# Retention and a squared-ReLU layer: the decay of q moved into GpSimd's cast, the retention outputs as plain copies by two engines

## Chip, cores, metric

One Trainium2 chip, one core. The metric is the device time of one execution in microseconds (us), lower is better.

## What is computed

```python
def attn_ref(q, k, v):            # (8, 8, 576, 64): batch, heads, sequence, head size
    scores = (1 / sqrt(64)) * q @ k.transpose(0, 1, 3, 2)
    gamma = 1 - 2.0 ** (-5 - arange(8))                 # one decay per head
    rel = pos[:, None] - pos[None, :]
    Dmat = where(rel >= 0, gamma[:, None, None] ** rel, 0)
    return (scores * Dmat) @ v

x = attn_ref(q, k, v).transpose(0, 2, 1, 3).reshape(4608, 512)
out = maximum(x @ w_in, 0) ** 2 @ w_out                 # w_in 512 x 2048, w_out 2048 x 512
```

Since gamma^(i-j) = gamma^i * gamma^-j, the decay can be applied as one factor on the side of the row i (q, or the finished output of row i) and one on the side of the column j (v).

## The kernel before

The work is cut into 36 units of 128 rows, taken in pairs (groups). Units 0 to 7 go another way that the change doesn't touch. A schedule written in Python runs through all tasks with assumed durations and emits each engine's instructions in the order that comes out, so a change of a task's engine or duration can also move other instructions.

GpSimd (POOL) casts k and q to float16 and multiplies v by its decay; a DMA transposes k and q:

```python
        def fq():
            sorted_cast(nc.gpsimd.tensor_copy, tile_of["kq", u][:, 1], tile_of["q32", u])

        def fv():
            t = tile_of["v16", u] = cast.tile([P, H, D], FP16, name="v16", tag="v16")
            nc.gpsimd.tensor_tensor(
                out=t, in0=tile_of["v32", u],
                in1=vdec[kind].rearrange("p (h o) -> p h o", o=1).to_broadcast([P, H, D]), op=ALU.mult)
        ...
        cq = add("POOL", base + 1, 0.62, fq, deps=[loaded["q", u], ck])
```

TensorE (PE) leaves the outputs of a pair in `psO`, a PSUM tile of two banks (`[P, 2, 512]`); the two units are the two halves of the columns. VectorE (DVE) takes both out and applies the row's decay:

```python
        for u in us:
            ...
                nc.vector.tensor_tensor(
                    out=tile_of["x", g][:, :, s * P:(s + 1) * P].rearrange("p n (c i) -> p c n i", c=2),
                    in0=tile_of["psO", g][:, :, cols(at)].rearrange("p c (n i) -> p c n i", i=64),
                    in1=gam[units[u][0]], op=ALU.mult)
```

`xT` then goes through the first product (`ph`), ScalarE's ReLU (`rl`), and the square (`gT`, on ScalarE or VectorE). The second product (`po`) is done with seven partial products instead of eight, for which VectorE makes sums and differences of squares, with two inputs in SBUF:

```python
                    nc.vector.tensor_tensor(out=Sx(k, h), in0=in0(h), in1=in1(h), op=op)   # gS
```

## Time and profile before

| | |
|---|---|
| median of 3 runs | 292.55 us (292.39 to 292.78) |
| span of the profiled run | 290.9 us, TensorE clock 1.0 |
| TensorE, VectorE, ScalarE, GpSimd busy | 283.0, 195.0, 187.5, 88.9 us |

A line of the timeline or the chain starts with its start and length in us. A line of the groups has, after the first bar, the busy time in us and the mean of one instruction in ns, then the idle time of the engine before them and what ended it. Matmuls overlap, so the distance from start to start tells more than busy time. Where this document speaks of steps, it is that distance on TensorE, and "lost" is what exceeds the median for its kind.

### The profile page before, as it was taken

Reading aid. Unit: us, or ns where it says so; the run is one execution under the profiler, and the core shown is the slowest. Engines: PE = TensorE matmul, PEld = TensorE weight load, DVE = VectorE, ACT = ScalarE, POOL = GpSimd, SP = SyncE. Lnnn points to the kernel's source line nnn. Section 1 sums busy time; section 2 is a strip of 40 time slices with the busy share of each in tenths; the row PEclk is TensorE's granted clock in tenths of the full one; section 3 lists DMA queues with packets and bytes.
Section 4 is the critical chain, followed back from the end, with each engine's and each line's share of the span. In section 5 each row is a group of like instructions: output and inputs, shape, how many; then the busy total and the mean of one; then the engine's idle time right before and its main releaser. Section 6 shows DMA issues by size and latency. Waiting matters only on the chain.

```text
span 290.9 us, 10062 instructions
## 1 busy us (share of the span) xinstructions
PE 283.0 (97%) x4328; PEld 234.0 (80%) x4328; DVE 195.0 (67%) x430; ACT 187.5 (64%) x354; POOL 88.9 (31%) x123
## 2 busy tenths in 40 slices
PE   7989999999999999999999999999999999999994
PEld 2557765688888888888888888888888888888883
DVE  3796589748485848656868857667786865565632
ACT  6456966296757575867666666766767676747830
POOL 5343454524434234251616041615151400000000
PEclk9999999999999999999999999999999999999999
DMA  7999999999999899997998599979896820201004
GB/s 201 327 368 387 370 276 250 239 220 186 233 214 214 185 148 247 221 186 189 196 208 180 126 192 211 202 183 180 211 188 171 159 74 2 74 3 72 2 2 144
DMA packets 139421, 54.13 MB, mean 186 GB/s; under 512 B 118129, under 2 KB 130929, under 8 KB 139377
## 3 DMA queue, kind: packets, MB, share of 16 engines
q1 hardware_dynamic: 139072, 53.23, 81.9%
q8 instruction: 34, 0.56, 0.9%
q10 hardware_dynamic: 304, 0.26, 0.3%
q14 instruction: 11, 0.08, 0.1%
HBM read 36.70 MB, written 9.44 MB: 159 GB/s over the span
## 4 chain that ended last, share of the span: by engine, by line
PE 89%; DMA 6%; SPq 1%; issue 1%; POOL 1%; DVE 0%; DVEq 0%; POOLq 0%
PE ph L827 42%; PE po L916 34%; PE po L865 5%; PE psO L343 4%; DMA wi<-in_moe_w_in_dram 3%; DMA pair<-in_q_dram 3%; PE psc L343 2%; PE psS L343 2%; SPq L298 1%; POOL w_in L322 1%; PE psT L418 1%; DVE o L939 0%; POOL qx L403 0%; DVE p L968 0%; DVEq L939 0%
## 5 line engine op out<-in xcount | busy, mean ns | idle before, releaser
L827 PE MATMUL ph<-xT,w_in 128*128 128x256 f16 x1152 | 139.4, 273 | 0.2 <-POOL w_in L322 0.2
L827 PEld LDWEIGHTS <-w_in 128*128 128x128 f16 x1152 | 111.1, 98 | 14.8 <-POOL w_in L322 0.4
L835 ACT ACTIVATE rl<-ph 128x512 f16<-128x512 f32 x144 | 84.3, 589 | 46.9 <-PE ph L827 45.0
L845 ACT ACTIVATE gT<-rl 128x512 f16<-128x512 f16 x104 | 65.6, 631 | 3.0
L916 PEld LDWEIGHTS <-gS 128*128 128x128 f16 x512 | 49.4, 98 | 6.1 <-DVE gS L893 0.2
L916 PE MATMUL po<-wT,gS 128*128 128x256 f16 x384 | 52.4, 273 | 0.0
L893 DVE TENSOR_TENSOR gS<-gT,gS 128x512 f16<-128x512 f16 x64 | 35.1, 554 | 11.6 <-ACT gT L845 11.0
L916 PEld LDWEIGHTS <-gT 128*128 128x128 f16 x384 | 37.2, 98 | 4.4
L893 DVE TENSOR_TENSOR gS<-gT 128x512 f16<-128x512 f16 x64 | 30.7, 481 | 12.9 <-ACT gT L845 12.9
L916 PE MATMUL po<-w_out,gT 128*128 128x256 f16 x256 | 34.5, 273 | 0.0
L355 POOL CAST kq<-q 128x512 f16<-128x512 f32 x28 | 18.8, 673 | 45.7 <-DMA q<-in_q_dram 45.5
L367 POOL TENSOR_TENSOR v<-v,vdec_full 128x512 f16<-128x512 f32 x24 | 26.2, 1093 | 19.6 <-DMA v<-in_v_dram 14.4
L355 POOL CAST kq<-k 128x512 f16<-128x512 f32 x28 | 18.6, 666 | 44.4 <-DMA k<-in_k_dram 41.7
L847 DVE TENSOR_TENSOR gT<-rl 128x512 f16<-128x512 f16 x40 | 18.9, 473 | 14.7 <-ACT rl L835 14.2
L929 ACT COPY u<-po 128x256 f32<-128x256 f32 x32 | 11.8, 369 | 20.4 <-PE po L916 20.4
L939 DVE TENSOR_TENSOR o<-po,u 128x256 f32<-128x256 f32 x31 | 13.0, 421 | 16.2 <-PE po L916 8.3
L704 DVE TENSOR_TENSOR xT<-psO,gam_full 128x512 f16<-128x512 f32 x28 | 18.9, 686 | 7.5 <-PE psO L343 7.4
L643 DVE TENSOR_TENSOR rT<-psc,mask 128x512 f16<-128x512 f32 x28 | 18.3, 683 | 5.5 <-PE psc L343 5.2
L916 PE MATMUL po<-w_out,gS 128*128 128x256 f16 x128 | 17.0, 273 | 0.0
L916 PE MATMUL po<-wT,gT 128*128 128x256 f16 x128 | 16.8, 273 | 0.0
L939 DVE TENSOR_TENSOR o<-po,p 128x256 f32<-128x256 f32 x17 | 7.2, 424 | 13.7 <-ACT u L929 7.1
L865 PE MATMUL po<-w_out,gT 128*128 128x512 f16 x64 | 15.8, 380 | 0.0
(81 smaller groups left out, 244.1 us busy)
## 6 DMA issues: line engine op xcount, KB each, us to landing
out_dram<-o SPq DMA_DIRECT2D x31, 256.0 KB, 3.0
k<-in_k_dram SPq DMA_DIRECT2D x24, 256.0 KB, 4.5
q<-in_q_dram SPq DMA_DIRECT2D x24, 256.0 KB, 4.8
v<-in_v_dram SPq DMA_DIRECT2D x24, 256.0 KB, 5.3
wi<-in_moe_w_in_dram SPq DMA_DIRECT2D x4, 1024.0 KB, 10.1
wo<-in_moe_w_out_dram SPq DMA_DIRECT2D x4, 1024.0 KB, 9.7
pair<-in_k_dram SPq DMA_DIRECT2D x4, 512.0 KB, 7.0
pair<-in_q_dram SPq DMA_DIRECT2D x4, 512.0 KB, 7.0
```

The source lines that it names most:

```text
L343: nc.tensor.matmul(out_, lhsT=lhsT, rhs=rhs, start=start, stop=True, skip_group_check=True, tile_position=(64 * row, 64 * col))
L355: op(out=out_.rearrange("p (n b a d) -> p n b a d", n=2, b=2, a=2), in_=in_.rearrange("p (n a b) d -> p n b a d", n=2, a=2))
L367: nc.gpsimd.tensor_tensor(out=t, in0=tile_of["v32", u], in1=vdec[kind].rearrange("p (h o) -> p h o", o=1).to_broadcast([P, H, D]), op=ALU. ...
L704: nc.vector.tensor_tensor(out=tile_of["x", g][:, :, s * P:(s + 1) * P].rearrange("p n (c i) -> p c n i", c=2), in0=tile_of["psO", g][:, :, ...
L827: nc.tensor.matmul(tile_of["ph", g, fb][:, j, :], lhsT=w_in16[:, m, fi * P:(fi + 1) * P], rhs=tile_of["x", g][:, m, :], start=(m == 0), st ...
L835: nc.scalar.activation(out=t, in_=tile_of["ph", g, fb], func=ACTF.Relu)
L845: nc.scalar.activation(out=t, in_=rl, func=ACTF.Square)
L847: nc.vector.tensor_tensor(out=t, in0=rl, in1=rl, op=ALU.mult)
L865: nc.tensor.matmul(tile_of["po", u], lhsT=tile_of["g", g][:, fi, s * P:(s + 1) * P], rhs=w_out16[:, fi, :], start=(fi == 0), stop=(fi == N ...
L893: nc.vector.tensor_tensor(out=Sx(k, h), in0=in0(h), in1=in1(h), op=op)
L916: nc.tensor.matmul(tile_of["pb", g, bank], lhsT=left(i), rhs=right[:, i, :], start=(start and i == 0), stop=(i == HF - 1), skip_group_chec ...
L939: nc.vector.tensor_tensor(out=o_tile(u)[:, half * HM:(half + 1) * HM], in0=bank(x), in1=tile_of[name, g], op=ALU.add)
```

## The change

VectorE has 28 multiplications out of PSUM in the changed form. The intent is to apply the row's decay earlier, in GpSimd's cast of q, where GpSimd has time, so that the outputs can leave PSUM as plain copies; then one unit of each pair can go to ScalarE, and the two copies could run side by side.

```diff
-    vdec = {}
+    vdec, qdec = {}, {}
 
     def make_vdec(kind, pos):
         t = const.tile([P, H], FP32, name=f"vdl_{kind}")
         nc.vector.tensor_scalar(out=t, in0=lnrow, scalar1=pos, scalar2=None, op0=ALU.mult)
+        if kind in ("full", "tail"):
+            e = qdec[kind] = const.tile([P, H], FP32, name=f"qdec_{kind}")
+            nc.scalar.activation(out=e, in_=t, func=ACTF.Exp, scale=-1.0)
...
-    gam = {"full": gam_f.rearrange("p n (c i) -> p c n i", c=2),
-           "tail": gam_f[:, :, 0:64].rearrange("p n (c i) -> p c n i", c=1).to_broadcast([P, 2, NP, 64])}
...
         def fq():
-            sorted_cast(nc.gpsimd.tensor_copy, tile_of["kq", u][:, 1], tile_of["q32", u])
+            for n in range(2):
+                nc.gpsimd.tensor_tensor(
+                    out=tile_of["kq", u][:, 1].rearrange("p (n b a d) -> p n b a d", n=2, b=2, a=2)[:, n],
+                    in0=tile_of["q32", u].rearrange("p (n a b) d -> p n b a d", n=2, a=2)[:, n],
+                    in1=qdec[kind].rearrange("p (n a b o) -> p n b a o", n=2, a=2, o=1)[:, n].to_broadcast([P, 2, 2, D]),
+                    op=ALU.mult)
...
-        cq = add("POOL", base + 1, 0.62, fq, deps=[loaded["q", u], ck])
+        cq = add("POOL", base + 1, 1.2, fq, deps=[loaded["q", u], ck] + tail)
...
-                nc.vector.tensor_tensor(
+                (nc.vector.tensor_copy if at else nc.scalar.copy)(
                     out=tile_of["x", g][:, :, s * P:(s + 1) * P].rearrange("p n (c i) -> p c n i", c=2),
-                    in0=tile_of["psO", g][:, :, cols(at)].rearrange("p c (n i) -> p c n i", i=64),
-                    in1=gam[units[u][0]], op=ALU.mult)
-            T["x", u] = add("DVE", key + at, 0.7, fx, deps=[t2] + ([T["x", us[at - 1]]] if at else []),
-                            acq=() if at else ("x",))
-        sched.free("prO", [T["x", us[-1]]])
+                    in_=tile_of["psO", g][:, :, cols(at)].rearrange("p c (n i) -> p c n i", i=64))
+            T["x", u] = add("DVE" if at else "ACT", key, 0.68 if at else 0.6, fx, deps=[t2], acq=() if at else ("x",))
+        sched.free("prO", [T["x", u] for u in us])
```

## The prediction

> **What bounds the kernel now.** I read the page's first part and chain, then TensorE's waits, then busy time by stretch, then the chain and the timeline of one pair of units.
>
> ```profile
> PE 283.0 (97%) x4328; PEld 234.0 (80%) x4328; DVE 195.0 (67%) x430; ACT 187.5 (64%) x354; POOL 88.9 (31%) x123
> PE 89%; DMA 6%; SPq 1%; issue 1%; POOL 1%; DVE 0%; DVEq 0%; POOLq 0%
> ```
>
> The first line is busy time by engine, the second the chain that ended last. TensorE (PE) is busy for 97% of the span and is 89% of the chain; VectorE (DVE), which the change relieves, is 0% of it. Busy alone proves little, since one 256-column matmul is recorded as 273 ns and neighbours overlap. So I looked at the pace, in the chain of one pair of units late in the run (start, length, what):
>
> ```profile
> 219.80 0.40 PE psO L343 x48
> 220.19 4.47 PE ph L827 x40
> 224.67 1.75 PE po L916 x16
> 226.41 1.31 PE ph L827 x12
> ```
>
> The pieces touch, and 1.75 us for 16 is 109 ns per matmul. Taking the start-to-start steps of all TensorE records, the median is 109 ns for both ph and po with 256 columns, and all steps that exceed the median of their kind by over 120 ns come to 11.2 us: 6.4 us in the first 30 us, 1.4 us in the next 30, and 3.4 us from 60 us to the end. Retention in the changed form (unit 8 onwards) lies in that last part, and most of those 3.4 us are steps of about 0.12 or 0.28 us at the switch between 64-row retention matmuls and full ones, and at a deliberate drain; none follows a wait for xT. TensorE's own list of waits says the same:
>
> ```profile
> PE warm L247 <- DVE junk L163: 1.3, 1, 1.3
> PE psO L343 <- DVE R L489: 0.9, 1, 0.9
> PE psT L418 <- DVE qx L403: 0.4, 1, 0.4
> PE psS L343 <- DVE vx L399: 0.3, 1, 0.3
> PE ph L827 <- POOL w_in L322: 0.2, 1, 0.2
> ```
>
> All five belong to the start and to units 0 to 7, which the change doesn't touch. **TensorE's issue rate is the bound**, at full clock, from about 57 us to the last product near 286 us.
>
> **What the Trainium skill says.** "TensorE: Matmul & The Clock Gate", section Back-to-back issue gap, gives an isolated warm gap of about N/2.4 + 2.5 ns, which is 109 ns for N = 256; the trace has 109, so nothing is left to gain inside a run of matmuls. (Its sustained 131 ns for N = 512 isn't met here: four po matmuls of 512 columns take 0.86 us.) "Perfetto Trace Analysis", section Identifying the Most-Contended Engine, warns that matmul busy time is a bad measure and names weight-load busy time and the arithmetic rate instead; weight loads are 80% here, which agrees with a saturated TensorE. "SBUF — State Buffer", section SBUF: two separate sides, says that GpSimd and a VectorE operation with two SBUF inputs take one port pair as an exclusive lock for the whole instruction. The trace agrees: gS sums (two SBUF inputs) take 419 ns on average where no GpSimd work overlaps, and 793 ns (gS from gT and gS) where GpSimd covers over half of them, up to 1259; xT, whose one input is PSUM, moves only from 690 to 714. "GPSIMD Engine Reference", section Elementwise — side-by-side cycle accounting, measured some 2.6 cycles an element for two-input work at 1.2 GHz, which would be 1.1 us for 512; the trace's v multiplication of 512 elements takes 1.04 us where nothing disturbs it, so they agree.
>
> **The change part by part.** 28 units (8 to 35) are in the changed form, in 14 pairs.
>
> ```profile
> L367 POOL TENSOR_TENSOR v<-v,vdec_full 128x512 f16<-128x512 f32 x24 | 26.2, 1093 | 19.6 <-DMA v<-in_v_dram 14.4 <-PE ph L827 3.5 <-PE psc L343 1.6
> L704 DVE TENSOR_TENSOR xT<-psO,gam_full 128x512 f16<-128x512 f32 x28 | 18.9, 686 | 7.5 <-PE psO L343 7.4
> L355 POOL CAST kq<-q 128x512 f16<-128x512 f32 x28 | 18.8, 673 | 45.7 <-DMA q<-in_q_dram 45.5
> L872 ACT COPY o<-po 128x512 f32<-128x512 f32 x4 | 2.4, 594 | 5.5 <-PE po L865 5.5
> L662 DVE CAST Rm<-psS 128x256 f16<-128x256 f32 x6 | 2.5, 412 | 0.0
> ```
>
> (After the bar: busy us, mean ns of one; then idle time before and its releasers.)
>
> VectorE loses 28 multiplications of 0.686 us and gets 14 plain copies. A copy out of PSUM isn't cheaper: 256 columns cost 412 ns as a cast, and the sums from PSUM with 256 columns cost 413 to 423. So a copy is taken as 0.68 us, and VectorE's saving is 28 x 0.686 - 14 x 0.68 = 9.7 us of 195.
>
> ScalarE gets 14 copies of 512 columns out of PSUM at 0.59 us: +8.3 us, from 187.5 to some 196.
>
> GpSimd's q cast becomes two multiplications of 256 columns. From casts (612 ns undisturbed for 512, 1041 for 1024) an element costs 0.84 ns and the start about 0.18 us; for the two-input v operation, (1043 - 183)/512 = 1.68 ns. One half is then 183 + 256 x 1.68 = 613 ns, two are 1.23 us (an estimate from these rows), against 0.617: +0.61 us a unit, +17 us in all, from 89 to 106 us.
>
> Two Exp activations on eight columns are added (0.3 us each); both fall in ScalarE's first 6 us, which the initial loads cover.
>
> **On or beside the path.** ScalarE had 10.2 us of work in each 15 us of the steady part, VectorE 11.4:
>
> ```profile
> 210.00:225.00 15.00, 15.00 (x254) 13.15 (x253) 11.38 (x23) 10.21 (x21) 5.23 (x7) 1.00 0.93 183
> 225.00:240.00 15.00, 15.00 (x245) 13.00 (x244) 11.82 (x24) 10.14 (x21) 3.98 (x5) 1.00 0.57 117
> ```
>
> (Stretch, its length, busy TensorE, weight loads, VectorE, ScalarE, GpSimd, clock, DMA.) With one pair in about 14.6 us, ScalarE rises to about 10.8 and VectorE falls to about 10.8 plus whatever the port lock adds. All stay under TensorE's 15. The retention outputs themselves have room before their reader:
>
> ```profile
> 220.31 0.69 DVE L704 TENSOR_TENSOR xT<-psO,gam_full 128x512 f16<-128x512 f32 x1 [0.43 <-PE psO L343]
> 222.17 0.68 DVE L704 TENSOR_TENSOR xT<-psO,gam_full 128x512 f16<-128x512 f32 x1
> 226.25 0.93 PE L827 MATMUL ph<-xT,w_in 128*128 128x256 f16 x7
> ```
>
> xT is whole at 222.85 and first read at 226.25. Over all 14 pairs that slack is 0.8 to 7.5 us, and running the two copies side by side can only widen it; the widening buys nothing, because TensorE has other matmuls queued ahead. The later q costs about 0.6 us before the transposing DMA; those transposes land 3.9 us (unit 9), and 6.9 us or more (all others), ahead of the first score matmul. So the sum on the path is **0 us**, and I predict 292.6 us against 292.55. The emitted order of the engines (compared between the two kernels) also shifts a few blocks of four or eight matmuls past each other, with the same number of matmuls; that is noise of a few tenths.
>
> **Rivals.**
> (a) ScalarE's extra 0.59 us a pair delays a bank's release or a Strassen intermediate. For: TensorE starts the product after the u copy as little as 0.30 us after that copy ends, and a ph bank is free as little as 0.24 us before it is reused. Against: the copy sits just after the retention outputs, where ScalarE had idled 1.98 us before its next rl. If each pair lost 0.1 to 0.2 us, that is 1.4 to 2.8 us: 294 to 295. The extreme, all 14 x 0.59, is 8.3 us, the only way I see to over 2% slower.
> (b) More GpSimd time holds the shared port and delays gS. For: the lock is visible, and one gS product starts only 0.86 us after its sum ends in the tightest group. Against: VectorE loses nearly 10 us of work at once. Worth +0 to 1 us.
> (c) VectorE's relief or the earlier xT removes TensorE waits. Even taking away all 3.4 us of steps from 60 us on gives 289.1, still 1.2% only; a realistic part is a few tenths. Over 2% faster (286.7) can't be had this way.
> (d) Loads: ld buffers are freed up to 0.6 us later, while the DMA engines are nearly full until 230 us. GpSimd waited 45.5 us for q, so it isn't the pacer; the room of several microseconds ahead of the scores takes it up.
>
> **Range and chances.** (a) and (b) lengthen, (c) shortens; each is most likely under 1 us. I take 291.4 to 294.2. Faster by over 2%: 0.01; within 2%: 0.97; slower: 0.02.
>
> **What would show it.** Right: TensorE still 109 ns a matmul and about 97% busy; xT on VectorE 14 times at 0.68 us and on ScalarE 14 times at 0.6 us; q multiplications 56 at about 0.61 us; VectorE near 186, ScalarE near 196, GpSimd near 106 us; span within 1.5 us. Wrong: ph or po waiting for ScalarE in every pair (a), gS means well over 554 and 481 ns with po waiting for them (b), psc waiting for the transposes (d), or a plain copy on VectorE much under 0.68 us.

## The result

The changed kernel takes 293.74 us (median of 4 runs, 293.58 to 294.48), the kernel before beside it 292.66 us. The ratio is 1.0042, with a 95% interval of 1.0021 to 1.0062. A ratio is the mean time of one kernel's fast runs over the mean of the other's of the same rounds, so it isn't quite the ratio of the medians. Two later repeats gave 1.0043 and 1.0047. So the change costs 1.2 to 1.4 us, within the predicted range (the second repeat's median, 294.35 us, lies just above it) and at 2% "the same", but clear of zero: the predicted 0 us on the path is not what happened.

The first lines of the page and of the chain, after the change:

```profile
PE 284.3 (97%) x4328; PEld 233.5 (80%) x4328; DVE 195.2 (67%) x416; ACT 195.7 (67%) x370; POOL 109.4 (37%) x151
PE 78%; DVE 7%; DMA 6%; ACT 4%; issue 1%; SPq 1%; POOL 1%; DVEq 0%; POOLq 0%
```

ScalarE rose as expected. **VectorE did not fall: 195.0 us before, 195.2 after**, although it has 14 instructions fewer. And the chain, 0% VectorE before, now runs 7% of the span through it (6% and 9% in the profiles of the two repeats). Where VectorE's time went shows in its groups. Before:

```profile
L893 DVE TENSOR_TENSOR gS<-gT,gS 128x512 f16<-128x512 f16 x64 | 35.1, 554 | 11.6 <-ACT gT L845 11.0
L893 DVE TENSOR_TENSOR gS<-gT 128x512 f16<-128x512 f16 x64 | 30.7, 481 | 12.9 <-ACT gT L845 12.9
```

After (with the lines of the changed parts):

```profile
L897 DVE TENSOR_TENSOR gS<-gT,gS 128x512 f16<-128x512 f16 x64 | 38.0, 598 | 12.8 <-ACT gT L849 12.2
L897 DVE TENSOR_TENSOR gS<-gT 128x512 f16<-128x512 f16 x64 | 34.3, 537 | 9.6 <-ACT gT L849 9.6
L365 POOL TENSOR_TENSOR kq<-q,qdec_full 128x256 f16<-128x256 f32 x48 | 32.8, 703 | 61.5 <-DMA q<-in_q_dram 61.5
L710 DVE CAST xT<-psO 128x512 f16<-128x512 f32 x14 | 9.7, 692 | 15.4 <-ACT xT L710 11.6 <-PE psO L344 3.8
L710 ACT CAST xT<-psO 128x512 f16<-128x512 f32 x14 | 8.2, 586 | 9.7 <-PE psO L344 8.5
```

Three readings. The same gS sums take 44 and 56 ns longer on average. The q multiplications take 703 ns on average, where 613 was predicted; those in the records that no two-input VectorE instruction overlaps have a median of 614. And VectorE sat idle for 11.6 us before its copies until **ScalarE's copy** had ended: the two don't run side by side. In the records, the second copy of a pair starts 31 to 34 ns after the first one's end, in all 14 pairs.

TensorE now waits for gS. From the list of waits of the weight loads, whose gS line had 0.2 us before:

```profile
PEld L920 <- DVE gS L897: 2.9, 6, 1.0
```

In the records of the kernel before, no step from 57 us on that leads to a ph or po matmul loses over 150 ns. In the changed kernel's profiled run six do, each ending with a gS sum, with 2.2 us lost in all; in the two profiles of the repeats it is three with 1.0 us and four with 1.5 us. (The first profiled run, 294.48 us, was the slowest of its four.) The worst place, first VectorE's and GpSimd's timelines before:

```profile
195.63 0.42 DVE L893 TENSOR_TENSOR gS<-gT,gS 128x512 f16<-128x512 f16 x1 [1.15 <-ACT gT L845]
195.97 0.42 DVE L893 TENSOR_TENSOR gS<-gT 128x512 f16<-128x512 f16 x1
196.30 0.83 DVE L893 TENSOR_TENSOR gS<-gT,gS 128x512 f16<-128x512 f16 x1
197.26 0.42 DVE L847 TENSOR_TENSOR gT<-rl 128x512 f16<-128x512 f16 x1
197.72 1.15 DVE L893 TENSOR_TENSOR gS<-gT,gS 128x512 f16<-128x512 f16 x1
...
196.22 0.64 POOL L355 CAST kq<-q 128x512 f16<-128x512 f32 x1 [5.68 <-DMA q<-in_q_dram]
197.53 1.05 POOL L367 TENSOR_TENSOR v<-v,vdec_full 128x512 f16<-128x512 f32 x1 [0.67 <-DMA v<-in_v_dram]
```

The same place after, with what TensorE's weight loads waited for:

```profile
196.27 0.85 DVE L897 TENSOR_TENSOR gS<-gT,gS 128x512 f16<-128x512 f16 x1 [1.56 <-ACT gT L849]
197.04 0.83 DVE L897 TENSOR_TENSOR gS<-gT 128x512 f16<-128x512 f16 x1
197.80 1.26 DVE L897 TENSOR_TENSOR gS<-gT,gS 128x512 f16<-128x512 f16 x1
198.98 0.82 DVE L851 TENSOR_TENSOR gT<-rl 128x512 f16<-128x512 f16 x1
199.84 0.89 DVE L897 TENSOR_TENSOR gS<-gT,gS 128x512 f16<-128x512 f16 x1
...
196.23 1.37 POOL L365 TENSOR_TENSOR kq<-q,qdec_full 128x256 f16<-128x256 f32 x2 [7.54 <-DMA q<-in_q_dram]
197.56 1.22 POOL L373 TENSOR_TENSOR v<-v,vdec_full 128x512 f16<-128x512 f32 x1
198.73 0.80 POOL L356 CAST kq<-k 128x512 f16<-128x512 f32 x1
...
200.78 0.33 PEld L920 LDWEIGHTS <-gS 128*128 128x128 f16 x4 [0.99 <-DVE gS L897]
```

Before, GpSimd paused 0.67 us between q and v, and VectorE could start a 0.42 us instruction in that gap. After, GpSimd has no gap from 196.2 to 199.5. The five VectorE instructions shown are the same ones in both: before they take 0.42, 0.42, 0.83, 0.42 and 1.15 us and are done in 3.2 us, after they take 0.82 to 1.26 us each and are done in 4.5 us, and the sum that TensorE needs is late. (They also begin 0.6 us later, about what TensorE had lost by then, so they meet GpSimd's work at another point.)

### The profile page after: what moved, and what is told of

Its sections match the earlier page's. It is cut to its first block, busy times and chain, and to the rows that moved or that the text cites. A ratio compares the mean times of both kernels' runs of the same rounds, so it can differ in the third digit from the quotient of the medians.

```text
span 292.8 us, 10092 instructions
## 1 busy us (share of the span) xinstructions
PE 284.3 (97%) x4328; PEld 233.5 (80%) x4328; DVE 195.2 (67%) x416; ACT 195.7 (67%) x370; POOL 109.4 (37%) x151
## 4 chain that ended last, share of the span: by engine, by line
PE 78%; DVE 7%; DMA 6%; ACT 4%; issue 1%; SPq 1%; POOL 1%; DVEq 0%; POOLq 0%
PE ph L831 34%; PE po L920 31%; PE po L869 5%; DVE gS L897 4%; PE psO L344 4%; DMA wi<-in_moe_w_in_dram 3%; DMA pair<-in_q_dram 2%; ACT gT L849 2%; PE psc L344 2%; PE psS L344 2%; ACT rl L839 2%; SPq L299 1%; DVE gT L851 1%; POOL w_in L323 1%; PE psT L424 1%
## 5 line engine op out<-in xcount | busy, mean ns | idle before, releaser
L920 PEld LDWEIGHTS <-gS 128*128 128x128 f16 x512 | 48.8, 98 | 8.8 <-DVE gS L897 2.9
L365 POOL TENSOR_TENSOR kq<-q,qdec_full 128x256 f16<-128x256 f32 x48 | 32.8, 703 | 61.5 <-DMA q<-in_q_dram 61.5
L897 DVE TENSOR_TENSOR gS<-gT,gS 128x512 f16<-128x512 f16 x64 | 38.0, 598 | 12.8 <-ACT gT L849 12.2
L897 DVE TENSOR_TENSOR gS<-gT 128x512 f16<-128x512 f16 x64 | 34.3, 537 | 9.6 <-ACT gT L849 9.6
L851 DVE TENSOR_TENSOR gT<-rl 128x512 f16<-128x512 f16 x40 | 21.1, 527 | 15.4 <-ACT rl L839 14.7
L356 POOL CAST kq<-k 128x512 f16<-128x512 f32 x28 | 19.7, 705 | 19.0 <-DMA k<-in_k_dram 18.5
L710 DVE CAST xT<-psO 128x512 f16<-128x512 f32 x14 | 9.7, 692 | 15.4 <-ACT xT L710 11.6
L710 ACT CAST xT<-psO 128x512 f16<-128x512 f32 x14 | 8.2, 586 | 9.7 <-PE psO L344 8.5
```

Of the source, the lines that this page charges most:

```text
L356: op(out=out_.rearrange("p (n b a d) -> p n b a d", n=2, b=2, a=2), in_=in_.rearrange("p (n a b) d -> p n b a d", n=2, a=2))
L365: nc.gpsimd.tensor_tensor(out=tile_of["kq", u][:, 1].rearrange("p (n b a d) -> p n b a d", n=2, b=2, a=2)[:, n], in0=tile_of["q32", u].rea ...
L851: nc.vector.tensor_tensor(out=t, in0=rl, in1=rl, op=ALU.mult)
L920: nc.tensor.matmul(tile_of["pb", g, bank], lhsT=left(i), rhs=right[:, i, :], start=(start and i == 0), stop=(i == HF - 1), skip_group_chec ...
```

## The experiments

Theory **L**: GpSimd's longer work that reads SBUF holds the port pair that VectorE's two-input instructions need, and late gS sums stop TensorE. Theory **W**: VectorE's copy waits for ScalarE's (or the reverse), so the freed VectorE time becomes waiting. Rivals: **O**, the order in which the schedule emits the engines' instructions; **D**, casts and loads that come later; **S**, ScalarE's load.

Each ratio is to the kernel before in the same rounds. The first four runs and the other eight were on two different chips.

### The q multiplication alone

The kernel before, with q multiplied by ones in two halves on GpSimd; order untouched, result right.

```diff
-            sorted_cast(nc.gpsimd.tensor_copy, tile_of["kq", u][:, 1], tile_of["q32", u])
+            for n in range(2):
+                nc.gpsimd.tensor_tensor(out=<q half n>, in0=<q32 half n>, in1=<ones half n, broadcast>, op=ALU.mult)
```

> The kernel before, in its own order of instructions, but GpSimd casts q of units 8 to 35 by two multiplications (by ones, so the result stays right) instead of one cast; VectorE still multiplies the retention outputs. Theory L (GpSimd's longer work holds the port pair that gS sums need, and TensorE waits for gS): 0.6 to 2.5 us slower than before, at least as much as the change itself (1.1 us), VectorE busy some 8 to 12 us longer than before although it has the same operations. Rival O (the shifted order of TensorE's blocks costs the time) and rival W (VectorE's copy waits for ScalarE's copy of the same PSUM tile): no change, within 0.3 us.

Measured: 293.79 us against 292.90, ratio 1.0024 (1.0012 to 1.0036). VectorE's busy time rose with exactly the same instructions:

```profile
PE 284.0 (97%) x4328; PEld 234.3 (80%) x4328; DVE 202.8 (69%) x431; ACT 187.5 (64%) x354; POOL 108.0 (37%) x151
```

From 195.0 to 202.8 us, for 19 us more of GpSimd work. (One instruction more than before is the memset of the ones.) L's sign and size are right, except that it isn't "at least as much as the change itself": 0.7 us, about half. Something else is needed.

### The order alone

The kernel before with the changed kernel's task engines and durations given to the schedule only; the operations stay on their engines.

```diff
-        cq = add("POOL", base + 1, 0.62, fq, deps=[loaded["q", u], ck])
+        cq = add("POOL", base + 1, 1.2, fq, deps=[loaded["q", u], ck] + tail)
...
-            T["x", u] = add("DVE", key + at, 0.7, fx, deps=..., acq=...)
+            T["x", u] = add("DVE" if at else "ACT", key, 0.68 if at else 0.6, fx, deps=[t2], acq=...)
```

> The operations of the kernel before, all of them, emitted in the order of the changed kernel on TensorE and the DMA queue. Rival O: about 1.1 us slower than before. Theory L and rival W: within 0.3 us of before.

Measured: 293.34 us, ratio 1.0019 (1.0000 to 1.0038), from 292.78 to 294.69 over six runs: two at the speed of before, one worse than the change. The profiled run was a fast one (292.82) and shows no wait for gS. Inconclusive; the reverse run below says more. The order does show in VectorE's busy time: 198.9 us, 3.9 more than before with the same instructions, since GpSimd's reading work now covers 59 of the 168 gS sums and VectorE squares for over half of their time instead of 45.

### The copies alone

The changed kernel with q cast plainly again, so without its decay. Its output is wrong, which doesn't matter for the time.

```diff
-            for n in range(2):
-                nc.gpsimd.tensor_tensor(... in1=qdec ...)
+            sorted_cast(nc.gpsimd.tensor_copy, tile_of["kq", u][:, 1], tile_of["q32", u])
```

> The changed kernel with q cast plainly in one instruction again, so without the decay of q: the result is wrong on purpose. Plain copies by ScalarE and VectorE, and the changed order, stay. Theory L: as fast as before or up to 0.6 us faster, VectorE busy some 10 us less than before. Rivals W and O: still about 1.1 us slower than before.

Measured: 293.51 us, ratio 1.0016 (1.0003 to 1.0030), so half a microsecond slower than before, not as fast. VectorE was busy for 191.9 us, 3 us less than before and not 10 (this run has the changed order, which alone had added 3.9), and idle for 10.6 us before its copies until ScalarE's had ended. L alone would have made this run no slower than before. W, or O, has a part too.

### Copies split by PSUM bank

ScalarE takes bank 0 of both units, VectorE bank 1. That alone left the wait in the built program (built, not run: the second copy waits for the semaphore of the first in all pairs); only with `psO` as two tiles of one bank each do both copies wait for TensorE alone. The other tiles that share its buffers (`psc`, `psS`) were split with it. `xT` is laid out by bank, and ph's output is written through a view that puts the rows back in order.

```diff
+    def out_banks(name):
+        return Banks([ps_ret.tile([P, 512], FP32, name=f"{name}{c}", tag=f"prO{c}") for c in range(2)])
...
-            tile_of["psO", g] = ps_ret.tile([P, 2, 512], FP32, name="psO", tag="prO")
+            tile_of["psO", g] = out_banks("psO")
...
-                    tile_of["x", g] = x_pool.tile([P, NP, n * P], FP16, name="xT", tag="xT")
+                    tile_of["x", g] = x_pool.tile([P, 2, NP, 2, 64], FP16, name="xT", tag="xT")
...
-                    out=tile_of["x", g][:, :, s * P:(s + 1) * P].rearrange("p n (c i) -> p c n i", c=2),
-                    in_=tile_of["psO", g][:, :, cols(at)].rearrange("p c (n i) -> p c n i", i=64))
+                    out=tile_of["x", g][:, at, :, w].rearrange("p n s i -> p s n i"),
+                    in_=tile_of["psO", g][:, at].rearrange("p (s n i) -> p s n i", s=2, i=64)[:, r])
```

> The changed kernel with the two PSUM banks of psO as two tiles: ScalarE copies one bank and VectorE the other, so neither waits for the other (right result). Rival W: the 1.1 us come back, within 0.3 us of before, no VectorE idle time before xT that ends with ScalarE's copy. Theory L: at most 0.4 us of it comes back; still 0.7 us or more slower than before.

Measured: right result, 293.48 us, ratio 1.0016 (1.0004 to 1.0029). Better than the 1.0042 of the change, but not back to before. As the change had been timed on other rounds, both went in again later, side by side on one chip:

> The kernel with the copies split by PSUM bank once more, now beside the changed kernel on the same chip. Rival W (waiting of one copy for the other): at least 0.5 us faster than the changed kernel beside it. Theory L: within 0.3 us of it.

> The changed kernel unchanged, for the comparison with the run split by bank: 1.002 to 1.006 of before.

Measured there: by bank 293.58 us, ratio 1.0018 (0.9999 to 1.0037); the change 294.35 us, ratio 1.0047 (1.0031 to 1.0064). The means are 293.44 and 294.27, so **0.8 us of the 1.4 us go with the split** (0.4 to 1.3 by the scatter of the six runs of each, an estimate), and 0.6 us remain. The waits before xT in that run, by bank:

```profile
ACT xT L722 <- PE psO L354: 8.1, 9, 1.8
DVE xT L722 <- PE psO L354: 7.7, 11, 1.4
```

ScalarE's copy is gone as a releaser of VectorE's. VectorE's busy time is 194.8 us as in the change: the port isn't helped by the split, which fits the 0.6 us that remain. In the profiles of the two by-bank runs TensorE still loses time at steps over 150 ns: 1.4 us in two steps that gS ends, and 1.0 us in three, two of which gS ends. W as I had put it first ("the 1.1 us come back") is wrong, though its later "at least 0.5 us faster" came true; L's "within 0.3 us" of the change is wrong: each holds for a part.

### More GpSimd work that reads, and as much that doesn't

The kernel before, with extra GpSimd work after each q cast, into a spare tile nobody reads: two multiplications that read q, or four memsets of about the same total time.

```diff
             sorted_cast(nc.gpsimd.tensor_copy, tile_of["kq", u][:, 1], tile_of["q32", u])
+            for n in range(2):                                   # first run
+                nc.gpsimd.tensor_tensor(out=spare[:, n], in0=<q32 half n>, in1=<ones, broadcast>, op=ALU.mult)
+            for n in range(4):                                   # second run
+                nc.gpsimd.memset(spare, 0.0)
```

> The kernel before with its own order, q cast plainly, and after each cast of units 8 to 35 two more GpSimd multiplications of 128 x 256 that read q and write a spare tile nobody uses: some 1.2 us of GpSimd work a unit (34 us in all) that reads SBUF, twice what the change added. Theory L (the shared port pair): VectorE's busy time rises by 8 us or more with the same operations, gS sums get longer, and the kernel is 0.7 to 3 us slower than before. If later casts and not the port are what costs (rival D), the same slowdown must show in the run with memsets.

> The same place and about the same GpSimd time a unit as the run before this one, but as four memsets of 128 x 256, which read nothing. Theory L, if only GpSimd work that reads SBUF blocks VectorE: gS sums as in the kernel before (means of 481 and 554 ns, within 30), time within 0.3 us of before. Rival D (the v cast and the loads come later): as slow as the run with reads. If memsets too hold the port pair, gS sums are as long as in the run with reads.

Measured with reads: 294.63 us, ratio 1.0063 (1.0034 to 1.0092). With memsets: 292.38 us, ratio 0.9983 (0.9966 to 0.9999). The first lines of the two pages, reads first:

```profile
PE 284.6 (97%) x4328; PEld 234.1 (80%) x4328; DVE 208.7 (71%) x431; ACT 187.6 (64%) x354; POOL 127.6 (44%) x179
```

```profile
PE 283.0 (97%) x4328; PEld 234.1 (81%) x4328; DVE 193.3 (67%) x430; ACT 187.5 (65%) x354; POOL 121.1 (42%) x235
```

Over 30 us of extra GpSimd work either way; VectorE pays 13.7 us in one and nothing in the other. The records of the memset run are sharper still. Of the gS sums and VectorE's squares, the 28 of which a memset alone covers over half take 416 ns on average, 426 at most; those that no GpSimd work touches take 421 ns; those that reading work covers over half take 736 ns. "SBUF — State Buffer", section SBUF: two separate sides, says that a VectorE instruction with two SBUF inputs contends only with a GpSimd instruction that reads SBUF, and this run agrees. Rival D is out: the memsets (34.9 us in all) delay v and what follows nearly as much as the reads (37.9 us). With L the dose counts: 19 us more of reading work cost 0.7 us, some 39 us cost 1.9 us.

### The changed operations in the old order

The changed kernel's operations with the schedule entries of the kernel before; TensorE's and the DMA queue's orders are then those of before.

```diff
-        cq = add("POOL", base + 1, 1.2, fq, deps=[loaded["q", u], ck] + tail)
+        cq = add("POOL", base + 1, 0.62, fq, deps=[loaded["q", u], ck] + tail)
...
-            T["x", u] = add("DVE" if at else "ACT", key, 0.68 if at else 0.6, fx, deps=[t2], acq=...)
+            T["x", u] = add("DVE", key + at, 0.7, fx, deps=[t2] + ([T["x", us[at - 1]]] if at else []), acq=...)
```

> The operations of the changed kernel, all of them, emitted in the order of the kernel before on TensorE and the DMA queue. Theory L alone: as slow as the changed kernel, 1.0028 to 1.006 of before. Rival O (order): within 0.3 us of before.

> The changed kernel unchanged, for its time on the same chip as these runs: 1.002 to 1.006 of before.

Measured: in the old order 294.18 us, ratio 1.0047 (1.0030 to 1.0064); the change itself 294.06 us, ratio 1.0043 (1.0026 to 1.0061). The shifted order isn't needed for the loss. VectorE was busy for 192.7 us in the old order, against 195.2 to 196.4 in the three profiles of the change: some 3 us of VectorE's time go with the order, without a difference in the kernel's time. Whether it has a share when the operations are the old ones stays open.

### Taking k off GpSimd

To give VectorE the port back, the k casts went to ScalarE: in the changed kernel all 28, in the kernel before every second one. The schedule knew of it.

```diff
-            sorted_cast(nc.gpsimd.tensor_copy, t[:, 0], tile_of["k32", u])
+            sorted_cast(nc.scalar.copy, t[:, 0], tile_of["k32", u])
...
-        ck = add("POOL", base, 0.65, fk, deps=[loaded["k", u]], acq=("kq",))
+        ck = add("ACT", base, 0.63, fk, deps=[loaded["k", u]], acq=("kq",))
```

> The changed kernel, with the k cast of units 8 to 35 moved from GpSimd to ScalarE (28 casts, some 0.6 us each), so that GpSimd's work that reads SBUF falls back to about that of the kernel before (some 91 us) while everything else of the change stays; the schedule knows of it. Theory L (shared port): VectorE's busy time falls to 185 to 190 us, and the kernel comes to 0.998 to 1.002 of before. Rival S (ScalarE's load is what costs the change its time): ScalarE rises to some 212 us and the kernel gets slower still than the change, over 1.006.

> The kernel before, with the k cast of every second unit from 8 on moved from GpSimd to ScalarE: the 8 us of ScalarE time that the change spends on copies, spent on taking work off GpSimd instead. Theory L: VectorE's busy time falls by 2 to 5 us, and the time is that of before or up to 0.5 us less, since TensorE already issues without a break; ratio 0.998 to 1.000. Rival S: 1.002 or more.

Measured: 296.77 us, ratio 1.0129 (1.0107 to 1.0152), and 295.14 us, ratio 1.0079 (1.0058 to 1.0100). Both are slower than either kernel, as S had it, and theory L's times are plainly missed. The first line of the page of the first one:

```profile
PE 284.4 (96%) x4328; PEld 233.9 (79%) x4328; DVE 186.4 (63%) x416; ACT 208.9 (71%) x398; POOL 87.8 (30%) x123
```

VectorE did fall to 186.4 us, as L expected of the port (and to 187.9 in the second run). But TensorE now waited for xT too, before ph. Of the 4.0 us that steps over 150 ns cost in the first run's profile, 1.6 us are three steps that xT ended, and 1.9 us still three that a gS sum ended: less load on the port and on VectorE did not by itself make the sums come in time. In the first run a ph matmul follows the end of its xT by 0.05 us in three pairs; in the second, three steps before ph, all ended by xT, lose 1.7, 0.8 and 0.2 us. In the second the scores of unit 16 start at 120.3 us instead of 117.5. So these kernels moved the order and the timing of the retention work as well as the casts; which of that and of ScalarE's queue does it, they don't tell. No version that I ran beats the kernel before: the memset run's interval ends just under 1, but it only adds work, and I take it as the same.

## Why the prediction was right, and which of its steps were not

"Within 2%" held for a reason that the prediction gave: TensorE issues one matmul after another at 109 ns (also after the change), its breaks from 60 us on are small, and no part of the change touches a matmul. That set a ceiling on the gain. It doesn't bound a loss: the run with all k casts on ScalarE has the same matmuls and lost 1.3%. The range held because room had been left in it for rivals (a) and (b); its likeliest time, 292.6 us, was 1.1 us too low. Of the signs of being wrong, (b)'s came true: gS means of 598 and 537 ns and po waiting for gS; and the span grew by 1.9 us, not by less than 1.5.

- **Sizes of the new work.** ScalarE was to reach some 196 us: 195.7. Its copy 0.59: 0.586. VectorE's copy 0.68: 0.692. An undisturbed q half 613 ns: 614. These held; disturbed, the q halves brought GpSimd to 109.4 us instead of 106.
- **"VectorE near 186".** Wrong: 195.2. The prediction knew the port lock and wrote "plus whatever the port lock adds", but gave that term no size and used, against rival (b), that "VectorE loses nearly 10 us of work at once". All of it came back: in the old order VectorE was busy for 192.7 us, so overlap with the longer q work gave back some 7 of the 9.7 us (q alone had added 7.8), and the rest comes with the shifted order. What could have been worked out: before, 45 of 168 gS sums and VectorE squares were covered for over half their time by GpSimd work that reads, and took 740 ns instead of 420. After, it is 68 of 168 at 760 ns. One reading beside it mixed two forms: "xT moves only from 690 to 714" takes in the slower multiplications of units 0 to 7; in the changed form alone it is 686 ns undisturbed and 689 ns covered (four of them), which makes its point more strongly.
- **"Running the two copies side by side can only widen" the slack of xT.** The first half is wrong: the copies run one after the other. The widening itself came (0.8 to 7.5 us before, 0.95 to 9.05 after, nearly as much in the run with the order alone) and bought nothing, as predicted. What was missed is that the wait lies in VectorE's own order of instructions: where ScalarE went first, in 11 of 14 pairs, VectorE's two multiplications of 0.69 us became 0.59 us of waiting plus a 0.69 us copy, 0.1 us less in all. The Trainium skill has a rule of this kind, in "PSUM — Partial Sum Buffer", section PSUM bank collisions raise a hardware error: reads of one bank by ScalarE and VectorE collide too, and the compiler puts a dependency between them. I had not asked which banks and tiles each copy reads; the built program's waits show it before anything runs. Here they go by tile: the program split by bank on one tile has the same waits, so no run shows what sharing a bank does by itself.
- **"0 us on the path".** This is the term of the sum that was mis-sized: 1.2 to 1.4 us. By the side-by-side run, 0.8 us goes away with the by-bank form and 0.6 us remains, close to the 0.7 us that the q multiplication costs alone. The parts tried alone (0.24% and 0.16%, the second with the changed order in it) add up to 0.40%, against 0.42 to 0.47% of the whole. The by-bank form also changed xT's layout and psO's tiles, so calling its 0.8 us the copies' mutual wait rests on that wait vanishing from the list, not on a run that changes it alone.
- **Rival (b), worth 0 to 1 us**: right in kind and size. **Rival (a)**, ScalarE delaying banks or intermediates: none of the long steps in the changed kernel's profiles ends with ScalarE. **Rival (d)**: the transposes still land 2.8 us or more ahead of the scores in the change's three profiles, where these tell the landing, and the memset run shows that later casts cost nothing.

Still open: the share of the emitted order in the runs with the old operations (1.0000 to 1.0038), and the split between waiting copies and order in the run with copies alone.

## What to carry to other kernels

Before giving GpSimd work to relieve VectorE, count VectorE's instructions with two SBUF inputs: GpSimd work that reads SBUF lengthens those it overlaps, and VectorE's busy time may not fall at all. Before splitting a copy out of PSUM between two engines, see that they read different tiles (and different banks), and look at the waits of the built program. TensorE issued almost without breaks here: no run gained from a VectorE with less to do (186.4 us at the least), while the two runs that only lengthened its sums lost 0.7 and 1.9 us.

## What the Trainium skill lacked or had wrong

- "SBUF — State Buffer": it says who blocks whom, and agrees; it lacks the size for short instructions. Here a 0.42 us two-input VectorE instruction takes 0.70 to 0.81 us on average, by run, when reading GpSimd work covers over half of it, up to 1.32 us, and a q half on GpSimd rises from 0.614 to 0.70 us on average in the changed kernel.
- "PSUM — Partial Sum Buffer": the rule is there, but not that the wait can cover a whole two-bank tile. Here copies of different banks of one tile still wait in the built program (not run); with a tile per bank they overlapped (in the second run, in the 13 pairs copied by one instruction each, the second copy started 0.40 to 0.67 us before the first's end in 12 and 0.27 us after it in one).
- "TensorE: Matmul & The Clock Gate": it gives 131 ns as the sustained step for 512 columns and some 81 ns for 128. Here the medians with a weight load for each matmul are 216 ns (512), 109 ns (256) and 56 ns (128), which is its isolated formula.
- "GPSIMD Engine Reference": some 2.6 cycles an element for two inputs (an estimate of 2.2 ns at its 1.2 GHz) and tens of cycles to dispatch an instruction. Here 512 elements take 1.04 us and 256 take 0.614; a line through the two gives 1.67 ns an element and 0.19 us to start, so a lower rate an element and a longer start.
